# Attention for batches 1 to 3 by halves of 64 tokens, with head and token on the partitions

## The chip, the cores and the metric

The kernel runs on one core of a Trainium2 chip. The metric is device time in microseconds (us) of one execution, the median of several; the profile is of one execution taken by the hardware profiler. The engines are named PE (TensorE: matrix products, its weight loads shown apart as PEld), DVE (VectorE), ACT (ScalarE), POOL (GpSimd) and SP (SyncE, which here issues all DMAs). Each engine works through its own queue in order; they meet at semaphores.

## The reference

q, k and v have 4 batches, 8 heads, 768 tokens and 64 dimensions per head, in fp32. Per head h there is a decay gamma = 1 - 2^(-5-h) and a recurrent state of 64 x 64:

```
state = gamma * state + k[t]^T v[t]
y[t]  = (1/8) * q[t] state
```

The eight heads' y are laid side by side (512 columns, 3072 rows of all batches), and a feed-forward stage follows: h = relu(y @ w_in) with 2048 columns, out = (h * h) @ w_out, 512 columns, fp32.

## The kernel before

The recurrence is done in chunks of C = 128 tokens, 24 in all (`chunks`, six per batch). q is scaled by gamma^t/8 and k by gamma^(-t) (`scale_q` L241, `scale_kv` L252), so that inside a batch the state is a plain sum. Heads go in pairs (NPAIR = 4): two heads of 64 dimensions fill the 128 partitions. For one chunk:

- `load_q`, `load_kv` (L78 to L91): DMAs from SP bring q for two chunks, and k and v for one, with tokens on the partitions: one DMA for k and one for v, 256 KB each.
- k is scaled on DVE into `ks`, v is cast on POOL into `v_bd`.
- q and k are transposed so that the dimensions of a pair lie on the partitions: for chunks below DMA_FROM = 8 by PE (L272, L286), from 8 on by DMAs (`dma_transpose_q` L300, `dma_transpose_k` L308). k is then put into a block-diagonal tile `k_bd`, one head of a pair in each half of the partitions (for DMA transposes by DVE, `spread_k` L314).
- `scores` (L323): two halves of four products each, k tokens x q tokens of one head (128 x 128), into PSUM tile `st`; DVE multiplies by the causal mask into `pt`.
- `state` (L347): four products (one per pair) add this chunk's k^T v to `c_ps`, a PSUM tile that lives through a batch; ACT and DVE each copy one half of the diagonal blocks into `s_bd`. The last chunk of a batch has none.
- `outputs` (L374): per pair one product with the state before the chunk (not in a batch's first chunk) and one per head with `pt`, twelve products into PSUM tile `y`; one ACT copy brings it into `xt` (L399).

All of these products have 128 moving columns. The feed-forward stage takes blocks of chunks (BLOCKS, four chunks and then two at a time) in pieces. A block of two has eight pieces of the first product (`first_product` L416, relu by ACT L428, square by DVE L412) and eight of the second (L478; every fourth ends with ACT's copy L488 and a store by SP L490). The pieces are numbered through the program. `put` hangs a step of attention on a piece's number, its place, and `before` (L611) emits the steps of a place right after that piece, then the squares that are due. So the order in every queue is written out by hand. `attend` (L573) gives the places of one chunk; for chunks from 8 on they are d-13 (scaling, k's transpose, load of chunk m+3), d-7, d-5, d-3 and d (outputs), with d = 55, 62, 70, then every 8 pieces; q's scaling and transposition come at d-15 or d-16. Places 33 to 40, 49 to 56, 65 to 72 and so on follow pieces of the first product, those between follow pieces of the second. PSUM has eight banks: one each for `tp`, `st`, `y` and `c_ps`, four for the feed-forward stage. At the start, before the first feed-forward work can run, `keep_awake` (L221) fills PE with idle products of 512 or 64 columns, each with its own weight load.

Of the kernel before, what the change touches and what calls it, by code (L numbers as in the profile page):

```python
# [20 lines left out]

DMA_FROM = 8


@with_exitstack
def kernel(
# [9 lines left out]
    nc = tc.nc  # L36
# [23 lines left out]
    qkpool = ctx.enter_context(tc.tile_pool(name="qkpool", bufs=4))  # L60
    qTpool = ctx.enter_context(tc.tile_pool(name="qTpool", bufs=3))
    kTpool = ctx.enter_context(tc.tile_pool(name="kTpool", bufs=2))
    ptpool = ctx.enter_context(tc.tile_pool(name="ptpool", bufs=2))
    xtpool = ctx.enter_context(tc.tile_pool(name="xtpool", bufs=2))
    hpool = ctx.enter_context(tc.tile_pool(name="hpool", bufs=2))
    wstage = ctx.enter_context(tc.tile_pool(name="wstage", bufs=5))
# [19 lines left out]
    def load_kv(m):  # L86
        b, i = chunks[m]
        for name, src, to in (("kn", k, raw_k), ("vn", v, raw_v)):
            t = ldpool.tile([P, H, D], FP32, name=name)
            nc.sync.dma_start(t[:], src[b, :, i * C : (i + 1) * C, :].rearrange("h s d -> s h d"))  # L90
            to[m] = t  # L91
# [33 lines left out]
    for h in range(H):  # L125
        nc.gpsimd.memset(lng[:, h : h + 1], float(np.log(gammas[h])))

    def exponents(pattern, step, name):
        ex_i = const.tile([P, NCH, H], I32, name=f"{name}_i")
        nc.gpsimd.iota(ex_i[:], pattern=pattern, base=0, channel_multiplier=step)  # L130
        ex_f = const.tile([P, NCH, H], FP32, name=f"{name}_f")
        nc.vector.tensor_copy(ex_f[:], ex_i[:])
        nc.vector.tensor_tensor(
            out=ex_f[:],
            in0=ex_f[:],
            in1=lng[:, None, :].to_broadcast([P, NCH, H]),
            op=ALU.mult,
        )
        return ex_f


    ex_q = exponents([[2 * C, NCH // 2], [1, 2], [0, H]], 2, "ex_q")
    ex_k = exponents([[C, NCH], [0, H]], 1, "ex_k")
    qf = const.tile([P, NCH, H], FP32)
# [27 lines left out]
    )  # L172


    v_bds = [const.tile([P, NPAIR, 4, D], BF16, name=f"v_bd{j}") for j in range(4)]
    k_bds = [const.tile([P, NPAIR, 2, C], BF16, name=f"k_bd{j}") for j in range(2)]
    s_bds = [const.tile([P, NPAIR, 2, D], BF16, name=f"s_bd{j}") for j in range(2)]
    def zero_on_scalar(out, rows=slice(0, P)):
# [59 lines left out]
    at = {m: {} for m in range(NCHUNK)}  # L238
    xts = {}

    def scale_q(m):  # L241
# [65 lines left out]

    def dma_transpose_k(m):  # L308
        a = at[m]
        kT = kTpool.tile([P, NPAIR, C], BF16, name="kT")  # L310
        nc.sync.dma_start_transpose(kT[:], a["ks"].rearrange("s h d -> s (h d)"))
        a["kT"] = kT

    def spread_k(m):  # L314
        a = at[m]
        kT = a.pop("kT")
        k_bd = k_bds[m % 2]
        for hh in range(2):
            rows = slice(64 * hh, 64 * (hh + 1))
            nc.vector.tensor_copy(k_bd[rows, :, hh, :], kT[rows])  # L320
        a["k_bd"] = k_bd

    def scores(m, half, pool=ps_st, name="st"):  # L323
# [23 lines left out]
    def state(m, on_scalar=1):  # L347
# [18 lines left out]
        for hh in range(2):  # L366
# [3 lines left out]
            else:  # L370
                nc.vector.tensor_copy(s_bd[rows, :, hh, :], c[rows, :, hh, :])

    def outputs(m):
        b, i = chunks[m]  # L374
        a = at.pop(m)
        tb = block_of[m]
        if m == first[tb]:
            xts[tb] = xtpool.tile([P, NCB, BLOCKS[tb] * C], BF16, name="xt")
        off = (m - first[tb]) * C
        y = ps_y.tile([P, NPAIR, C], FP32, name="y")  # L380
# [23 lines left out]

    squares = []

    def take_squares():
        while squares:  # L410
            hv = squares.pop(0)
            nc.vector.tensor_mul(hv, hv, hv)  # L412

    h2s = {}

    def first_product(tb, hp, f, cols):  # L416
# [16 lines left out]
    def first_unit(tb, g, c, parts=(0, 1)):  # L433

        if tb not in h2s:
            h2s[tb] = hpool.tile([P, NFB, 4 * C], BF16, name="h2")
        if (tb, g, c) not in open_ps:
            open_ps[tb, g, c] = ps_f.tile([P, FPQ, C], FP32, name="psf")
        hp = open_ps[tb, g, c]
        cols = slice(c * C, (c + 1) * C)  # L440
        half = FPQ // 2
        for part in parts:
            for fq in range(part * half, (part + 1) * half):
                first_product(tb, hp[:, fq, :], g * FPQ + fq, cols)
        if 1 in parts:
            relu(h2s[tb][:, g * FPQ : (g + 1) * FPQ, cols], open_ps.pop((tb, g, c)))

    def ffn_pieces(tb):
        nch = BLOCKS[tb]
        TB = nch * C  # L450
        if tb == 0:
            for f in range(FPQ, NFB):
                hp = ps_f.tile([P, TB], FP32, name="psf")
                first_product(tb, hp[:], f, slice(0, TB))
                relu(h2s[tb][:, f, :], hp)
                yield
# [6 lines left out]
        else:  # L463
            h2s[tb] = hpool.tile([P, NFB, 4 * C], BF16, name="h2")
            per = 512 // TB
            for f0 in range(0, NFB, per):
                hp = ps_f.tile([P, per, TB], FP32, name="psf")
                for f in range(f0, f0 + per):
                    first_product(tb, hp[:, f - f0, :], f, slice(0, TB))
                relu(h2s[tb][:, f0 : f0 + per, :TB], hp)  # L470
                yield

        h2 = h2s.pop(tb)

        def second(op, j, g, cols=slice(0, DM)):
            for fq in range(FPQ):
                f = g * FPQ + fq
                nc.tensor.matmul(  # L478
                    op[:],
                    lhsT=h2[:, f, j * C : (j + 1) * C],  # L480
                    rhs=w_out_bf[g][:, fq, cols],
# [4 lines left out]
        def store(op, j, cols=slice(0, DM)):  # L486
            osb = opool.tile([P, cols.stop - cols.start], FP32, name=f"osb{cols.stop - cols.start}")
            nc.scalar.activation(osb[:], op[:], AF.Copy)  # L488
            r0 = (first[tb] + j) * C
            nc.sync.dma_start(out[r0 : r0 + C, cols], osb[:])  # L490

# [80 lines left out]

    def attend(m, scaled, places):  # L573
        by_dma = m >= DMA_FROM
        if m % 2 == 0:
            put(scaled, scale_q, m)
            put(scaled if by_dma else places[0], dma_transpose_q if by_dma else transpose_q, m)
        put(places[0], scale_kv, m)
        if by_dma:
            put(places[0], dma_transpose_k, m)  # L580
        put(places[1], spread_k if by_dma else transpose_k, m)
        put(places[2], scores, m, 0)
        put(places[3], scores, m, 1)
        put(places[3], state, m)
        put(places[4], outputs, m)

    put(6, load_w_out, 2)
# [10 lines left out]
    attend(5, None, (27, 29, 31, 33, 35))  # L598
    attend(6, 30, (33, 35, 37, 39, 42))
    attend(7, None, (40, 42, 44, 46, 49))  # L600

# [4 lines left out]
    for m, d in zip(range(8, NCHUNK), done):  # L606
        attend(m, d - 15 if d < 70 else d - 16, (d - 13, d - 7, d - 5, d - 3, d))
        if m + 3 < NCHUNK:
            put(d - 13, load, m + 3)
# [43 lines left out]
```

## Time and profile before

| | us |
|---|---|
| median of 3 runs (221.71 to 222.68) | 221.72 |
| the profiled execution | 221.87 |
| its span, first to last instruction | 220.1 |
| PE busy | 211.2 |
| DVE busy | 127.0 |
| ACT busy | 116.4 |
| POOL busy | 30.6 |

The profiled execution's own time is 1.8 us longer than its span. The granted TensorE clock was full in every stretch. In a row of the timeline the columns are start, length, engine, line, operation, what is written from what, how many neighbours are merged, and in brackets the idle time of the engine before it with what ended it. In a row of the table by stretches each engine's busy time is followed by its number of instructions; the last three columns are the granted clock, the DMA share and GB/s. DVE's scaling of k takes 716 ns, its mask 692 ns, its square 437 ns; ACT's relu takes 596 ns, the copy into `xt` 746 ns; ACT's state copy takes 373 ns and DVE's 427 ns; POOL's cast of v 662 ns. A k transposition by DMA lands 2.4 us after its issue, one of q 4.3 us.

### The profile page before, as it was taken

To read this page: it belongs to the slowest core of one execution; us is meant where nothing else is said; L and a number is where in the kernel's file an instruction comes from. 1 tells how busy PE (TensorE), PEld (TensorE's weight loads), DVE (VectorE), ACT (ScalarE), POOL (GpSimd) and SP (SyncE) were. 2 spreads that over 40 slices of the span, in tenths; PEclk is the share of its full clock that TensorE was granted. 3 is DMA by queue.
4 is the path that set the end of the run, shared out by engine and by line. 5 is a ranking of instruction groups with operands and counts; after the bars stand their busy time and mean duration, and the time that the engine had idled before them with its cause. 6 is when DMAs were issued, how large, how long until landed. Compare 5 with 4: busy or idle time off the path is not lost.

```text
span 220.1 us, 4737 instructions
## 1 busy us (share of the span) xinstructions
PE 211.2 (96%) x1920; PEld 148.9 (68%) x1943; DVE 127.0 (58%) x257; ACT 116.4 (53%) x206; POOL 30.6 (14%) x66
## 2 busy tenths in 40 slices
PE   6798999999999999999999999999999999999994
PEld 1466744556975975875975975975975975975853
DVE  4857789362495683682783783782783783751320
ACT  8564788338853653652653643652643643642631
POOL 3213435542111110101100101100101000000000
PEclk9999999999999999999999999999999999999999
DMA  6999999999998996397395398396398222201102
GB/s 152 238 231 369 388 374 232 362 246 216 288 236 132 259 157 132 115 231 155 99 228 136 114 209 182 87 236 155 93 209 191 71 51 71 74 0 48 51 0 95
DMA packets 87925, 38.05 MB, mean 173 GB/s; under 512 B 67808, under 2 KB 81376, under 8 KB 87904
## 3 DMA queue, kind: packets, MB, share of 16 engines
q1 hardware_dynamic: 87904, 37.76, 73.0%
q8 instruction: 15, 0.25, 0.5%
q14 instruction: 6, 0.05, 0.1%
HBM read 27.26 MB, written 6.29 MB: 152 GB/s over the span
## 4 chain that ended last, share of the span: by engine, by line
PE 92%; DMA 2%; ACT 1%; SPq 1%; DVE 1%; issue 1%; ACTq 0%
PE psf L419 38%; PE psf L478 37%; PE y L391 5%; PE st L331 4%; DMA kn<-in_k_dram 2%; PE y L383 2%; PE c_ps L357 2%; SPq L90 1%; PE psf L226 1%; PE tp L277 1%; PE tp L290 1%; DVE ks L255 1%; ACT xt L399 0%; PE psf L331 0%; PE y L226 0%
## 5 line engine op out<-in xcount | busy, mean ns | idle before, releaser
L419 PE MATMUL psf<-xt,w_in_bf 128*128 128x256 bf16 (+2 forms) x879 | 91.3, 259 | 0.6 <-ACT xt L399 0.4
L478 PE MATMUL psf<-w_out_bf,h 128*128 128x512 bf16 (+2 forms) x378 | 88.5, 370 | 1.0
L419 PEld LDWEIGHTS <-w_in_bf 128*128 128x128 bf16 x880 | 72.4, 98 | 13.6 <-issue 0.5
L428 ACT ACTIVATE h<-psf 128x512 bf16<-128x512 f32 x96 | 57.0, 596 | 26.1 <-PE psf L419 24.8
L478 PEld LDWEIGHTS <-h 128*128 128x128 bf16 x400 | 37.0, 98 | 34.5
L338 DVE TENSOR_TENSOR pt<-st,cmask 128x512 bf16<-128x512 f32 x44 | 30.4, 692 | 42.8 <-PE st L331 42.2
L412 DVE TENSOR_TENSOR h<-h 128x512 bf16<-128x512 bf16 x96 | 40.9, 437 | 23.9 <-ACT h L428 22.4
L263 POOL CAST v_bd<-vn 128x512 bf16<-128x512 f32 x24 | 15.9, 662 | 127.2 <-DMA vn<-in_v_dram 123.4
L488 ACT ACTIVATE osb<-psf 128x512 f32<-128x512 f32 (+2 forms) x25 | 14.4, 580 | 27.4 <-PE psf L478 24.3
L399 ACT ACTIVATE xt<-y 128x512 bf16<-128x512 f32 x24 | 17.9, 746 | 19.0 <-PE y L391 18.3
L331 PEld LDWEIGHTS <-k_bd 128*128 128x128 bf16 x192 | 14.1, 98 | 7.3 <-ACT k_bd L297 1.2
L391 PE MATMUL y<-pt,v_bd 128*128 128x128 bf16 x192 | 18.2, 219 | 0.0
L369 ACT ACTIVATE s_bd<-c_ps 64x256 bf16<-64x256 f32 x24 | 9.0, 373 | 17.2 <-PE c_ps L357 16.9
L331 PE MATMUL st<-qT,k_bd 128*128 128x128 bf16 x176 | 17.5, 220 | 0.5 <-DVE k_bd L295 0.5
L255 DVE TENSOR_TENSOR ks<-kn,kf 128x512 bf16<-128x512 f32 x24 | 17.2, 716 | 0.2
L391 PEld LDWEIGHTS <-v_bd 128*128 128x128 bf16 x192 | 14.5, 98 | 2.4 <-issue 0.7
L244 DVE TENSOR_TENSOR qs<-qn,qf 128x1024 bf16<-128x1024 f32 x12 | 15.0, 1253 | 1.4 <-DMA qn<-in_q_dram 1.4
L320 DVE COPY k_bd<-kT 64x512 bf16<-64x512 bf16 x32 | 9.1, 286 | 10.4 <-DMA kT<-ks 9.9
L383 PE MATMUL y<-qT,s_bd 128*128 128x128 bf16 x80 | 14.5, 219 | 0.1
L226 PE MATMUL psf<-ident 128*128 128x512 bf16 (+1 forms) x48 | 8.8, 326 | 2.1 <-POOL ident L152 2.1
L297 ACT ACTIVATE k_bd<-tp 64x512 bf16<-64x512 bf16 x12 | 7.0, 587 | 4.7 <-PE tp L290 4.5
L383 PEld LDWEIGHTS <-s_bd 128*128 128x128 bf16 x80 | 7.8, 98 | 1.2
(45 smaller groups left out, 78.9 us busy)
## 6 DMA issues: line engine op xcount, KB each, us to landing
qn<-in_q_dram SPq DMA_DIRECT2D x12, 512.0 KB, 4.7
kn<-in_k_dram SPq DMA_DIRECT2D x24, 256.0 KB, 5.1
vn<-in_v_dram SPq DMA_DIRECT2D x24, 256.0 KB, 5.5
out_dram<-osb SPq DMA_DIRECT2D x23, 256.0 KB, 3.3
w_stage<-in_moe_w_out_dram SPq DMA_DIRECT2D x4, 1024.0 KB, 10.2
w_stage<-in_moe_w_in_dram SPq DMA_DIRECT2D x3, 1024.0 KB, 10.9
w_stage<-in_moe_w_in_dram SPq DMA_DIRECT2D x2, 512.0 KB, 6.5
kT<-ks SPq DMA_TRANSPOSE x16, 2.4
```

Of the source, the lines that this page charges most:

```text
L244: nc.vector.tensor_tensor(out=qs[:], in0=raw_q.pop(m).rearrange("s h r d -> s r h d"), in1=qf[:, i : i + 2, :, None].to_broadcast([P, 2, H ...
L255: nc.vector.tensor_tensor(out=ks[:], in0=raw_k.pop(m)[:], in1=kf[:, i, :, None].to_broadcast([P, H, D]), op=ALU.mult,)
L263: nc.gpsimd.tensor_copy(v_bd[:, :, ::3, :], vn.rearrange("s (p hh) d -> s p hh d", hh=2))
L331: nc.tensor.matmul(st[:, pp, hh, :], lhsT=a["k_bd"][:, p, hh, :], rhs=a["qT"][:, :, p, :], start=True, stop=True,)
L338: nc.vector.tensor_tensor(out=a["pt"][:, 2 * half : 2 * half + 2], in0=st[:], in1=cmask.rearrange("s r t -> s (r t)")[:, None, None, :].to ...
L383: nc.tensor.matmul(y[:, p, :], lhsT=s_bds[(m - 1) % 2][:, p], rhs=a["qT"][:, :, p, :], start=True, stop=False,)
L391: nc.tensor.matmul(y[:, p, :], lhsT=a["v_bd"][:, p, 2 * hh : 2 * hh + 2, :], rhs=a["pt"][:, p, hh, :], start=(i == 0 and hh == 0), stop=(h ...
L399: nc.scalar.activation(xts[tb][:, :, off : off + C].rearrange("e p (s r) -> e p r s", r=2), y.rearrange("e p (r s) -> e p r s", r=2), AF.Copy,
L412: nc.vector.tensor_mul(hv, hv, hv)
L419: nc.tensor.matmul(hp, lhsT=w_in_bf[g][:, cb, fq * 128 : (fq + 1) * 128], rhs=xts[tb][:, cb, cols], start=(cb == 0), stop=(cb == NCB - 1),)
L428: nc.scalar.activation(hv, hp[:], AF.Relu)
L478: nc.tensor.matmul(op[:], lhsT=h2[:, f, j * C : (j + 1) * C], rhs=w_out_bf[g][:, fq, cols], start=(f == 0), stop=(f == NFB - 1),)
```

## The change

It concerns chunks 6 to 23, which are batches 1 to 3. The loads of k and v put token and head of a pair together on the partitions: partition 64 * hh + s holds token s of a half chunk for head hh of each pair, and the free dimension counts half u and pair p (eight groups of 64). That takes four DMAs of 64 KB for k and four for v. A chunk is then worked in two halves u of 64 tokens:

- `scale_k2`: two DVE instructions, one for each half of the partitions, write the scaled k into a block-diagonal tile `ks_bd2s`; its other blocks were zeroed once.
- `cast_v2`: three POOL casts, one into `v2` and one for each half of the partitions into the block-diagonal `v_bd2s`.
- `transpose_k2`: the block-diagonal k is transposed whole, eight blocks of 128 x 128: by one DMA from chunk 8 on, by PE for chunks 6 and 7, with one copy by ACT and one by DVE. `spread_k` is gone.
- `scores2`: eight products of 64 columns into one `st`, one mask on DVE.
- `state2`, once for each half: four products of 64 columns, then the two copies into `s_bd`, of which there are now three.
- `outputs2`, once for each half: eight products of 64 columns (four in a batch's first half) and one ACT copy of that half. Both halves stand at one place and write one PSUM tile `y`.

Constants for it are made at place 8 (`pack_constants`), and ten zeroings on DVE stand at places 10 to 19. The tile of h is cut into tiles of 4096 columns, three buffers for the former two of twice the size.

```diff
-    hpool = ctx.enter_context(tc.tile_pool(name="hpool", bufs=2))
+    hpool = ctx.enter_context(tc.tile_pool(name="hpool", bufs=3))
...
+                pairs = rows.rearrange("(p hh) (u s) d -> hh s u p d", hh=2, u=2)
+                for hh in range(2):
+                    for u in range(2):
+                        nc.sync.dma_start(
+                            t[64 * hh : 64 * (hh + 1), u * NPAIR : (u + 1) * NPAIR, :],
+                            pairs[hh, :, u],
+                        )
...
+    def zero_off_diagonal(t, hh):
+        nc.vector.memset(t[halves[hh], :, 1 - hh, :], 0.0)
...
+    def scale_k2(m):
+        b, i = chunks[m]
+        ks = ks_bd2s[m % 2]
+        kn = raw_k.pop(m)
+        for hh, rows in enumerate(halves):
+            nc.vector.tensor_tensor(
+                out=ks[rows, :, hh, :],
+                in0=kn[rows],
+                in1=kf2[rows, i].rearrange("s u p -> s (u p)")[:, :, None].to_broadcast(
+                    [64, 2 * NPAIR, D]
+                ),
+                op=ALU.mult,
+            )
+        at[m]["ks"] = ks
+
+    def cast_v2(m):
+        vn = raw_v.pop(m)
+        v2 = v2pool.tile([P, 2 * NPAIR, D], BF16, name="v2")
+        nc.gpsimd.tensor_copy(v2[:], vn[:])
+        v_bd = v_bd2s[m % 2]
+        for hh, rows in enumerate(halves):
+            nc.gpsimd.tensor_copy(v_bd[rows, :, hh, :], vn[rows])
+        at[m].update(v2=v2, v_bd=v_bd)
+
+    def transpose_k2(m):
+        a = at[m]
+        kT = kTpool.tile([P, 2 * NPAIR, C], BF16, name="kT")
+        if m >= DMA_FROM:
+            nc.sync.dma_start_transpose(kT[:], a["ks"].rearrange("s c hh d -> s (c hh d)"))
+        else:
+            tp = ps_tp.tile([P, 2 * NPAIR, C], BF16, name="tp")
+            for c in range(2 * NPAIR):
+                nc.tensor.transpose(tp[:, c, :], a["ks"][:, c], ident[:])
+            nc.scalar.activation(kT[:, 0:NPAIR], tp[:, 0:NPAIR], AF.Copy)
+            nc.vector.tensor_copy(kT[:, NPAIR:], tp[:, NPAIR:])
+        a["kT"] = kT
+
+    def half_of(qT, p, u):
+        return qT[:, :, p, u * (C // 4) : (u + 1) * (C // 4)]
+
+    def scores2(m):
...
+        for u in range(2):
+            for p in range(NPAIR):
+                c = u * NPAIR + p
+                nc.tensor.matmul(
+                    st[:, c, :], lhsT=kT[:, c, :], rhs=half_of(a["qT"], p, u),
...
+        nc.vector.tensor_tensor(out=pt[:], in0=st[:], in1=cmask2..., op=ALU.mult)
+
+    def state2(m, u):
...
+        for p in range(NPAIR):
+            nc.tensor.matmul(
+                c[:, p, :],
+                lhsT=a["ks"][:, u * NPAIR + p],
+                rhs=a["v2"][:, u * NPAIR + p, :],
...
+        s_bd = s_bds[(2 * m + u) % 3]
+        nc.scalar.activation(s_bd[halves[0], :, 0, :], c[halves[0]], AF.Copy)
+        nc.vector.tensor_copy(s_bd[halves[1], :, 1, :], c[halves[1]])
+
+    def outputs2(m, u):
...
+        if u == 0:
+            xt_of(m)
+            a["y"] = ps_y.tile([P, NPAIR, 2, C // 2], FP32, name="y")
+        y = a["y"]
...
+        for p in range(NPAIR):
+            inter = i > 0 or u > 0
+            if inter:
+                nc.tensor.matmul(
+                    y[:, p, u, :],
+                    lhsT=s_bds[(2 * m + u - 1) % 3][:, p],
+                    rhs=half_of(a["qT"], p, u),
...
+            nc.tensor.matmul(
+                y[:, p, u, :],
+                lhsT=a["v_bd"][:, u * NPAIR + p],
+                rhs=a["pt"][:, u * NPAIR + p, :],
...
+        nc.scalar.activation(
+            xts[tb][:, :, off : off + C // 2].rearrange("e p (s r) -> e p r s", r=2),
+            y[:, :, u, :].rearrange("e p (r s) -> e p r s", r=2),
+            AF.Copy,
+        )
...
+    def attend2(m, q_at, places):
+        attend_q(m, *q_at)
+        put(places[0], scale_k2, m)
+        put(places[0], cast_v2, m)
+        put(places[1], transpose_k2, m)
+        put(places[2], scores2, m)
+        put(places[3], state2, m, 0)
+        put(places[4], state2, m, 1)
+        for u in range(2):
+            put(places[5], outputs2, m, u)
...
-    attend(6, 30, (33, 35, 37, 39, 42))
-    attend(7, None, (40, 42, 44, 46, 49))
+    put(8, pack_constants)
+    for j, t in enumerate(ks_bd2s + v_bd2s):
+        for hh in range(2):
+            put(10 + 2 * j + hh, zero_off_diagonal, t, hh)
+    for hh in range(2):
+        put(18 + hh, zero_off_diagonal, s_bds[2], hh)
+    attend2(6, (30, 32), (32, 35, 38, 39, 40, 42))
+    attend2(7, (None, None), (39, 42, 45, 46, 47, 49))
...
-        attend(m, d - 15 if d < 70 else d - 16, (d - 13, d - 7, d - 5, d - 3, d))
+        q_at = (d - 15 if d < 70 else d - 16,) * 2
+        attend2(m, q_at, (d - 13, d - 13, d - 5, d - 4, d - 2, d))
```

## The prediction

> **What bounds the kernel now.** I read the page's engine totals and its chain of waits first: is one engine the limit, and where? PE (matrix products) is busy 96% and makes up 92% of the chain. So a change counts by what it takes from PE's queue and by any moment for which PE stops.
>
> ```profile
> span 220.1 us, 4737 instructions
> PE 211.2 (96%) x1920; PEld 148.9 (68%) x1943; DVE 127.0 (58%) x257; ACT 116.4 (53%) x206; POOL 30.6 (14%) x66
> PE 92%; DMA 2%; ACT 1%; SPq 1%; DVE 1%; issue 1%; ACTq 0%
> ```
>
> Next the table by stretches of 10 us, for the stage that the change rewrites. PE has no idle time there (its 78 to 96 records are long products); DVE is at half to two thirds.
>
> ```profile
> 120.00:130.00 10.00, 9.90 (x96) 8.38 (x96) 6.96 (x15) 6.47 (x12) 0.61 (x1) 1.00 0.70 178
> 130.00:140.00 10.00, 9.95 (x78) 6.35 (x77) 4.62 (x10) 3.29 (x7) 1.23 (x2) 1.00 0.87 160
> ```
>
> Then the timeline, for the pace of PE. A row merges neighbours and holds the drain of the last one (0.22 us for 128 columns, 0.19 for 64; the shortest rows). Four products of 128 columns: (0.39 - 0.22)/3 = 56 ns each. The warm-up products of 64 columns, each with its own weight load: (0.86 - 0.19)/23 = 29 ns. So 64 columns cost half of 128, loads included.
>
> ```profile
> 13.64 0.86 PE L226 MATMUL psf<-ident 128*128 128x64 bf16 x24
> 132.06 0.39 PE L331 MATMUL st<-qT,k_bd 128*128 128x128 bf16 x4
> ```
>
> Last, two places where two engines read different parts of one PSUM tile. The transposes end at 15.11; ACT copies one half of `tp` at 15.15; DVE, idle for 1.34 us, starts on the other half at 15.78, after ACT's end, and ACT is named as releaser. The second pair does the same on disjoint partitions. No data passes between them: in this program accesses of different engines to one PSUM bank go one after the other, whatever columns they touch.
>
> ```profile
> 14.49 0.62 PE L277 MATMUL tp<-ident,qs 128*128 128x128 bf16 x8
> 15.15 0.60 ACT L280 ACTIVATE qT<-tp 128x512 bf16<-128x512 bf16 x1 [0.56 <-PE tp L277]
> 15.78 0.42 DVE L281 COPY qT<-tp 128x512 bf16<-128x512 bf16 x1 [1.34 <-ACT qT L280]
> ...
> 17.36 0.59 ACT L297 ACTIVATE k_bd<-psf 64x512 bf16<-64x512 bf16 x1 [1.61 <-PE psf L290]
> 17.98 0.43 DVE L295 COPY k_bd<-psf 64x512 bf16<-64x512 bf16 x1 [1.18 <-ACT k_bd L297]
> ```
>
> **The change, part by part.** It concerns chunks 6 to 23, three batches of six.
>
> *PE's own work.* Before: scores 8 x 18, state 4 x 15, outputs 12 x 18 - 4 x 3 = 408 products of 128 columns, at 56 ns 22.8 us. After: scores2 8 x 18, state2 8 x 18 - 4 x 3, outputs2 16 x 18 - 4 x 3 = 552 of 64 columns, at 29 ns 16.0 us. Chunks 6 and 7 have four more transposes each, 8 x 56 ns = 0.4 us. All of it is on the path: -6.4 us. Bounds: 27 ns a product (half of 56 less a little) gives -7.5; 56 ns gives +8.5.
>
> The Trainium skill speaks against this in "TensorE: Matmul & The Clock Gate", section Back-to-back issue gap: in streams of weight load and product the load shares in the pace, and 128 columns sustain about 81 ns. The trace disagrees (56 ns with loads, 29 ns for 64 columns). By an estimate from that page's figure, 552 products at 81 ns would take 44.7 us, and the sum below would be 266.
>
> *outputs2: two halves in one bank, at one place.* `y` is one tile of 512 fp32, a bank. Half 0's eight products write it, ACT copies half 0, then half 1's eight products write other columns of the same bank. By the rows above PE must wait for ACT's copy, and nothing else in PE's in-order queue can go ahead. The copy of half the columns: 128x512 takes 0.746 us, ACT's 64x256 from PSUM 0.373; half of the former plus its share of fixed cost is 0.45 (from 596 and 373 ns for 512 and 256 elements the fixed part is 0.15; the strided rest 0.6 halves to 0.3). Bounds 0.37 and 0.75.
>
> ```profile
> 85.82 0.22 PE L383 MATMUL y<-qT,s_bd 128*128 128x128 bf16 x1
> 86.69 0.74 ACT L399 ACTIVATE xt<-y 128x512 bf16<-128x512 f32 x1 [1.80 <-PE y L391]
> ...
> 94.13 0.22 PE L383 MATMUL y<-qT,s_bd 128*128 128x128 bf16 x1
> 94.33 0.60 ACT L428 ACTIVATE h<-psf 128x512 bf16<-128x512 f32 x1 [0.28 <-PE psf L419]
> 95.00 0.75 ACT L399 ACTIVATE xt<-y 128x512 bf16<-128x512 f32 x1
> ```
>
> At 85.82 (a place in the second products) ACT is free: eight products 0.20, drain 0.19, ACT's start 0.04, copy 0.45, PE's start 0.05, against 0.23 without the wait: 0.70 us. At 94.13 (first products) the relu of the piece just done is ahead on ACT until 94.93: copy 95.00 to 95.45, PE at 95.50 instead of 94.36: 1.14 us, say 1.1. Places 49, 55, 70, 86 ... (nine) lie in first products, 42, 62, 78, 94 ... (nine) in second: 9 x 1.1 + 9 x 0.7 = +16.2 us. Bounds 14.8 and 21.6 by the copy's; 0 if PE doesn't wait.
>
> *state2: two passes over one accumulator.* Pass 1 adds to the PSUM columns that pass 0's copies are reading, so PE must wait for both copies, ACT's 0.373 then DVE's 0.427; before, a whole chunk (8 us) lay between. Passes stand two pieces apart (1.75 us), one in chunks 6 and 7. DVE's queue decides. In an even chunk, from PE's arrival at scores2: mask 0.44 to 1.13, both scale_k2 of the next chunk to 2.56, a square to 3.00, DVE's state copy to 3.43. PE reaches pass 1 at 0.23 + 0.87 + 0.12 + 1.75 = 2.97 and goes on at 3.48: 0.5 us. In an odd chunk there is no square and PE arrives at 2.93; DVE's copy ends at 2.99: 0.1. Sum 8 x 0.5 + 5 x 0.1 (the last chunk of a batch has no pass 1) + 2 x 0.3 (chunks 6 and 7: drain 0.19, copies 0.37 + 0.11 + 0.43, less a piece of 0.86) = +5.1 us. Bounds 0 (copies always in time) and +16 (rival below).
>
> *DVE and ACT otherwise.* DVE a chunk: one mask instead of two (-0.69), no spreading of k (-0.57), scale_k2 two instructions of 64 partitions and the same length (+0.72), one state copy more (+0.43): even. ACT: 0.45 x 2 instead of 0.75, one state copy more: +0.5 of 8 us. Both stay under 70%: nothing beyond the waits above.
>
> *POOL:* three casts of 0.61 instead of one, 1.8 of 8 us; they wait for loads and freed buffers, not for PE. Nothing, unless beside DVE (rival).
>
> *SP and DMA.* SP issues per block of two chunks 16 loads instead of 4, and k transposes of q's size. Before a block takes 16.6 us, after about 18. Issues: k 2 x 1.5 (like q's 1.5), q's own 1.5 + 0.57, two stores 0.36 each, loads 16 x 0.33 (the shortest store) to 0.57 (the median k load): 11.1 to 14.9 us. It fits. A kT lands like qT, 4.3 us (3.1 to 5.5) after issue instead of 2.4; it is issued some 2.6 us after its place, scores2 needs it eight pieces later (8 us): covered by about 1 us. Nothing; if the cover goes, the wait is one for one.
>
> *Setting up, places 8 to 19.* pack_constants is small operations on idle POOL (1.78 us idle at 27.07) and 0.5 us of DVE. The ten memsets, 8 x 0.27 + 2 x 0.14 = 2.4 us, go into DVE just where it runs without a break (31.99 to 37.39), ahead of the scaling of q for chunk 4.
>
> ```profile
> 38.04 1.22 DVE L244 TENSOR_TENSOR qs<-qn,qf 128x1024 bf16<-128x1024 f32 x1
> 40.32 0.61 PE L277 MATMUL tp<-ident,qs 128*128 128x128 bf16 x8
> ```
>
> That ends at 39.26 and PE takes it at 40.32; 2.2 us later less 0.3 of idle time, PE waits about +0.9 us. Bounds 0 and 1.5.
>
> The tiles of h are cut in halves and use three buffers: no wait on them before, none after, 0.
>
> Sum: -6.4 + 16.2 + 5.1 + 0.9 = +15.8. The profiled execution took 221.87 (span 220.1 and 1.8 around it): 237.7. The median of the runs is 0.15 lower: 237.5.
>
> **The rivals.**
>
> *PE doesn't wait in outputs2* (accesses of PE and ACT to different columns of a bank are let run together). The rows show ACT against DVE, none shows a PE write against a reader of other columns. Then 237.5 - 16.2 = 221.3, no change; if the state copies are in time too, 216. It is the other side, and decides where each of the 18 waits is under 0.02 us (0.3 us with the state waits gone). Chance 0.10. The Trainium skill, "PSUM — Partial Sum Buffer", section PSUM bank collisions raise a hardware error, wants PSUM guarded by bank and 32-partition group, not by address; by that rule the wait stays, as both halves use all partitions.
>
> *DVE is late because POOL casts beside it.* At 39.17 a k scaling took 1.10 us instead of 0.68 beside a POOL cast. Twice 0.42 for the 13 chunks with a scaling ahead of the state copy: +10.9, 248. Against: POOL's buffers come free six pieces earlier, so the casts should be over. Chance 0.06.
>
> *SP becomes the bound.* At 133.09 a k load took 0.84 us to issue; 16 x 0.84 + 5.8 = 19.2 a block against 18.1: 8 x 1.1, 246. It decides from 0.77 us an issue. Against: 0.57 and 0.53 where nothing is queued. Chance 0.05.
>
> *Products of 64 columns take as long as 128* (the weights then set the pace): 8.5 instead of -6.4, 252. Against: the 24 warm-up products; for: these all loaded one matrix. Chance 0.05.
>
> **How the numbers follow.** The forecast has 0.74, and 237.5 is its time. Its range by the bounds is 229 to 244 (state waits gone and copies of 0.37 us: 231, memsets hidden and 27 ns a product as well: 229; copies of 0.75 us and 1.5 us at the memsets: 243.5). I give 228 to 245; left out are the first rival and those above 245, under 2 in 10 with what the forecast has in its own tails. What tells from no change is about 0.5%, 1.1 us. The first rival, spread over 216 to 224, gives faster 0.05 and same 0.04; the forecast's tail 0.01 of each. Slower 0.89.
>
> **What would show it.** Right: PE idle 0.7 or 1.1 us between the two halves of each chunk's outputs, released by ACT's xt copy; smaller idle time before state2's second pass, released by DVE's s_bd copy; 64-column products 29 ns apart; loads of k and v issued in 0.35 to 0.6 us. Wrong: ACT's copy of half 0 overlapping half 1's products, PE waiting for kT, or a wait before the transposes at 40 us that isn't there.

## The result and the profile after

The changed kernel takes 241.82 us (median of four runs, 241.61 to 243.74) where the kernel before, measured beside it, takes 221.74: a ratio of 1.0914 (95% interval 1.0852 to 1.0976). It is slower, as forecast, and 4.3 us above the forecast of 237.5, inside the range of 228 to 245.

The profiled execution took 241.61 us, with a span of 239.5 and 2.1 us around it. So the span grew by 19.4 us, and what lies around it by 0.3. The page's totals and its chain of waits, the first views that were read of the kernel before:

```profile
span 239.5 us, 5316 instructions
...
PE 212.8 (89%) x2095; PEld 145.4 (61%) x2095; DVE 130.4 (54%) x257; ACT 123.1 (51%) x241; POOL 57.9 (24%) x115
...
PEclk9999999999999799999999999999999999999999
...
PE 74%; ACT 10%; DVE 9%; DMA 4%; issue 2%; ACTq 0%; DVEq 0%
```

PE fell from 96% to 89% busy and from 92% to 74% of the chain. No other engine of this line filled up, but the issuing of DMAs, which is SP's work, isn't counted in it; the rest of the chain is now handed from engine to engine. Two of the 10 us stretches in the rewritten stage say the same (columns: the stretch and its length; then busy us with the number of records of PE, PEld, DVE, ACT, POOL; granted clock; DMA share; GB/s). PE, which had no idle time in such stretches, now stands still for about 1 us in 10:

```profile
140.00:150.00 10.00, 9.15 (x85) 5.56 (x85) 4.64 (x9) 4.04 (x9) 2.49 (x4) 1.00 0.84 193
150.00:160.00 10.00, 8.93 (x100) 7.49 (x99) 6.33 (x12) 6.10 (x12) 2.70 (x4) 1.00 0.59 147
```

The list of waits names what for (total us, times, the longest). Those for `y`, the state copies and q had been forecast, that for kT had not:

```profile
PE y L539 <- ACT xt L553: 12.3, 18, 0.9
PE st L488 <- DMA kT<-ks_bdp: 3.6, 2, 3.4
PE c_ps L515 <- DVE s_bd L525: 2.3, 8, 0.4
...
PE tp L323 <- DVE qs L290: 1.6, 3, 0.8
```

These figures leave out the time in which a product's drain overlaps its successor. Taken instead from the start of each product to the start of the next, less the product's usual pace, the span's growth comes apart like this:

| part | forecast us | measured us | from |
|---|---|---|---|
| PE's own products | -6.4 | -6.4 | counts times pace; 29 ns for 64 columns |
| `y`: PE waits for the copy of half 0 | +16.2 | +15.2 | 18 waits: 0.96 to 1.08 in first products, 0.70 in second |
| state2: second pass | +5.1 | +3.8 | 7 x 0.43, 0.56 at 64 us, 0.23 at 72 us; nothing in odd chunks |
| q of chunk 4 and the zeroing | +0.9 | +0.95 | one wait at 41.34 us |
| kT late | 0 | +3.9 | 3.5 at 79.95 us, 0.4 at 169.85 |
| clock behind the late kT | - | +1.6 | 4.0 us at a granted 0.60 |
| w_in at 33.7 us | - | +0.1 | one wait |
| sum | +15.8 | +19.2 | span: +19.4 |

The timeline shows the first of these waits in a place in first products and then one in second products (start, length, engine, line, operation, tiles; in brackets the idle time before it and what ended it). At 139.31 the eighth product of half 0 is issued, but ACT has a relu ahead of the copy of `y`; PE goes on at 140.31. At 148.14 ACT is free and PE goes on at 148.87:

```profile
139.31 0.60 ACT L597 ACTIVATE h<-psf 128x512 bf16<-128x512 f32 x1 [0.28 <-PE psf L588]
139.31 0.19 PE L546 MATMUL y<-pt,v_bdp 128*128 128x64 bf16 x1
...
139.80 0.45 ACT L553 ACTIVATE xt<-y 128x256 bf16<-128x256 f32 x1
140.31 0.19 PE L539 MATMUL y<-qT,s_bd 128*128 128x64 bf16 x1 [0.80 <-ACT xt L553]
```

```profile
148.14 0.19 PE L546 MATMUL y<-pt,v_bdp 128*128 128x64 bf16 x1
148.87 0.19 PE L539 MATMUL y<-qT,s_bd 128*128 128x64 bf16 x1 [0.54 <-ACT xt L553]
```

What had not been forecast lies at 80 us. The first of the following fences holds PE's rows in the timeline, the second the stretches around them:

```profile
75.54 1.06 PE L588 MATMUL psf<-xt,w_in_bf 128*128 128x128 bf16 x16
79.95 0.41 PE L488 MATMUL st<-qT,kT 128*128 128x64 bf16 x8 [3.35 <-DMA kT<-ks_bdp]
80.19 1.36 PE L588 MATMUL psf<-xt,w_in_bf 128*128 128x128 bf16 x16
```

```profile
76.60:80.00 3.40, 0.05 (x2) 0.06 (x3) 0.00 (x0) 0.60 (x1) 0.45 (x1) 1.00 0.82 170
80.00:84.00 4.00, 4.00 (x51) 4.00 (x52) 1.87 (x4) 1.35 (x3) 0.00 (x0) 0.60 0.41 90
```

PE stands still for 3.4 us until the transposed k of chunk 8 lands. Then its clock is granted at a mean of 0.60 over 4 us: the same sixteen products take 1.36 us instead of 1.06, and 4.0 x 0.40 = 1.6 us are lost after the wait is over. In the Trainium skill, "TensorE: Matmul & The Clock Gate", Part 1 on the HAM clock gate, PE goes to half its clock after an idle window of about 3.4 us and comes back after about as long a time of sustained work; the trace agrees with it, with an idle time of 3.4 us and half the clock from 80.75 to 84.2 us, 3.5 us in all. The 3.4 us aren't a sharp bound in these runs, though: in the run with half 1 a place later the clock also fell to half at a wait of 2.6 us, and it stayed there for 6.9 us.

Why kT is late is seen in SP's queue. Its rows in one block of two chunks:

```profile
139.08 1.31 SPq L468 DMA_TRANSPOSE kT<-ks_bdp  x1
140.44 0.60 SPq L87 DMA_DIRECT2D qn<-in_q_dram  x1
141.10 2.62 SPq L102 DMA_DIRECT2D kn<-in_k_dram  x4
143.82 2.59 SPq L102 DMA_DIRECT2D vn<-in_v_dram  x4
146.52 1.26 SPq L349 DMA_TRANSPOSE qT<-qs  x1
147.89 1.24 SPq L468 DMA_TRANSPOSE kT<-ks_bdp  x1
149.17 2.92 SPq L102 DMA_DIRECT2D kn<-in_k_dram  x4
152.19 3.09 SPq L102 DMA_DIRECT2D vn<-in_v_dram  x4
155.38 1.02 SPq L658 DMA_DIRECT2D out_dram<-osb  x2
156.50 1.33 SPq L468 DMA_TRANSPOSE kT<-ks_bdp  x1
```

Each row begins within about 0.1 us of the end of the one before it. From one kT at 139.08 to the one two chunks later at 156.50 SP needs 17.4 us, and the sixteen loads of 64 KB take 11.2 of them, 0.70 each. Over five blocks, from kT of chunk 9 at 85.46 to that of chunk 19 at 174.51, it needs 17.8 us a block; a block of PE's takes 17.9, and from 21 to 193 us SP never pauses for more than 0.44 us. Its queue is full. In the kernel before it wasn't: here SP pauses for 1.0 us ahead of qT and 1.8 us ahead of kT, which leaves at once when its k is scaled (148.40):

```profile
141.98 0.57 SPq L90 DMA_DIRECT2D kn<-in_k_dram  x1
142.65 1.36 SPq L90 DMA_DIRECT2D vn<-in_v_dram  x1
144.98 1.69 SPq L303 DMA_TRANSPOSE qT<-qs  x1
148.42 1.39 SPq L311 DMA_TRANSPOSE kT<-ks  x1
```

In the changed kernel the scaling of the k that the transpose at 147.89 moves had ended at 145.58. In 14 of the 16 chunks from chunk 8 on, kT leaves 0.1 to 0.2 us after SP's last instruction. In twelve of them that is 2 to 3 us after its data was ready, in chunk 8, the first whose k is transposed by DMA, 6.5 us, and in chunk 9 10.6 us. So SP, not the scaling, sets when k is transposed.

### The profile page after: what moved, and what is told of

It reads as the page before. It is cut to its first block, busy times and chain, and to the rows that moved or that the text cites. A ratio compares the mean times of both kernels' runs of the same rounds, so it can differ in the third digit from the quotient of the medians.

```text
span 239.5 us, 5316 instructions
## 1 busy us (share of the span) xinstructions
PE 212.8 (89%) x2095; PEld 145.4 (61%) x2095; DVE 130.4 (54%) x257; ACT 123.1 (51%) x241; POOL 57.9 (24%) x115
## 4 chain that ended last, share of the span: by engine, by line
PE 74%; ACT 10%; DVE 9%; DMA 4%; issue 2%; ACTq 0%; DVEq 0%
PE psf L646 32%; PE psf L588 29%; ACT h L597 5%; ACT xt L553 3%; DMA kT<-ks_bdp 3%; PE y L539 2%; PE c_ps L515 2%; PE st L488 2%; DVE h L568 2%; DVE qs L290 2%; DVE s_bd L525 2%; DMA qn<-in_q_dram 2%; PE y L546 1%; PE y L425 1%; PE tp L323 1%
## 5 line engine op out<-in xcount | busy, mean ns | idle before, releaser
L495 DVE TENSOR_TENSOR pt<-st,cmask 128x512 bf16<-128x512 f32 x18 | 12.4, 691 | 40.0 <-PE st L488 39.5
L461 POOL CAST v_bdp<-vn 64x512 bf16<-64x512 f32 x36 | 23.5, 653 | 40.8 <-PE y L546 39.7
L458 POOL CAST v<-vn 128x512 bf16<-128x512 f32 x18 | 13.3, 739 | 81.9 <-issue 56.0
L553 ACT ACTIVATE xt<-y 128x256 bf16<-128x256 f32 x36 | 16.3, 454 | 20.3 <-PE y L546 20.3
L445 DVE TENSOR_TENSOR ks_bdp<-kn,kf 64x512 bf16<-64x512 f32 x36 | 25.9, 719 | 0.6
L539 PE MATMUL y<-qT,s_bd 128*128 128x64 bf16 x132 | 12.1, 192 | 12.3 <-ACT xt L553 12.3
L525 DVE CAST s_bd<-c_ps 64x256 bf16<-64x256 f32 x33 | 14.1, 428 | 11.4 <-ACT s_bd L524 10.7
L524 ACT ACTIVATE s_bd<-c_ps 64x256 bf16<-64x256 f32 x33 | 12.3, 372 | 14.2 <-PE c_ps L515 14.1
L546 PEld LDWEIGHTS <-v_bdp 128*128 128x128 bf16 x144 | 9.7, 97 | 15.3 <-issue 14.0
L546 PE MATMUL y<-pt,v_bdp 128*128 128x64 bf16 x144 | 12.9, 193 | 0.0
L515 PE MATMUL c_ps<-v,ks_bdp 128*128 128x64 bf16 x132 | 9.3, 194 | 2.4 <-DVE s_bd L525 2.3
```

The source lines that it names most:

```text
L445: nc.vector.tensor_tensor(out=ks[rows, :, hh, :], in0=kn[rows], in1=kf2[rows, i].rearrange("s u p -> s (u p)")[:, :, None].to_broadcast([6 ...
L461: nc.gpsimd.tensor_copy(v_bd[rows, :, hh, :], vn[rows])
L515: nc.tensor.matmul(c[:, p, :], lhsT=a["ks"][:, u * NPAIR + p], rhs=a["v2"][:, u * NPAIR + p, :], start=(i == 0 and u == 0 and p == 0), sto ...
L525: nc.vector.tensor_copy(s_bd[halves[1], :, 1, :], c[halves[1]])
L539: nc.tensor.matmul(y[:, p, u, :], lhsT=s_bds[(2 * m + u - 1) % 3][:, p], rhs=half_of(a["qT"], p, u), start=True, stop=False,)
L546: nc.tensor.matmul(y[:, p, u, :], lhsT=a["v_bd"][:, u * NPAIR + p], rhs=a["pt"][:, u * NPAIR + p, :], start=not inter, stop=True,)
```

## The experiments

All edits are to the changed kernel, except where the kernel before is named. Ratios are to the kernel before, measured beside each, with 95% intervals.

**Half 1 of the outputs in a bank of its own.** The second half of `y` takes a buffer from the pool of `tp`, so that no product writes to a bank that ACT is reading.

```diff
-            a["y"] = ps_y.tile([P, NPAIR, 2, C // 2], FP32, name="y")
-        y = a["y"]
+            y = ps_y.tile([P, NPAIR, 2, C // 2], FP32, name="y")
+        else:
+            y = ps_tp.tile([P, NPAIR, 2, C // 2], FP32, name="tp")
```

> Half 1 of each chunk's outputs is written into the bank of tp, half 0 stays in y; nothing else differs from the changed kernel. Theory (PE waits because both halves lie in one PSUM bank): the 18 waits for ACT's xt copy, 15.3 us in the changed kernel's trace, go, and the time falls to 241.8 - 15.3 = 226.5 us (225 to 228). Rival (ACT is simply late there, and PE would wait for it at the next step that needs it): the idle time moves to another line and the time stays within 5 us of 241.8.

Measured: 238.23 us, ratio 1.0728 (1.0672 to 1.0785). The 18 waits for ACT's copy are gone, but only 3.6 of their 15.2 us came off the time. The line of the waits, and one chunk in the timeline, SP's row and PE's:

```profile
PE st L488 <- DMA kT<-ks_bdp: 12.5, 11, 3.8
```

```profile
154.41 1.02 SPq L659 DMA_DIRECT2D out_dram<-osb  x2
155.54 1.32 SPq L468 DMA_TRANSPOSE kT<-ks_bdp  x1
159.90 0.41 PE L488 MATMUL st<-qT,kT 128*128 128x64 bf16 x8 [1.27 <-DMA kT<-ks_bdp]
```

PE now waits for kT in 11 chunks, 14.3 us from start to start. The chunk shown had its k scaled by 152.57; the transpose left at 155.54, when SP had issued the loads and stores ahead, and PE had its scores at 159.90. The mechanism of the wait is as forecast; its price in this kernel isn't, because SP's queue takes as long as before: from kT of chunk 9 to that of chunk 19 it is 89.1 us, with the `y` waits and without them. A wait of 0.8 us is new: chunk 7's transposes, which use the bank of `tp`, wait for ACT's copy out of it.

**Half 1 a place later.** The same wait is removed in another way: a piece of the feed-forward stage's products, some 0.9 us, is put between the two halves. In chunks 6 and 7, half 1 then reads the v of chunks 8 and 9, which is cast into the same tile by then, so those parts of the output are others.

```diff
-            put(places[5], outputs2, m, u)
+            put(places[5] + u, outputs2, m, u)
```

> Both halves in one bank as in the changed kernel, but half 1 one piece of feed-forward work (0.87 us) after half 0. Theory: the wait is as long as ACT's copy and the relu ahead of it, 0.7 to 1.1 us, so a piece in between hides nearly all of it: 15.3 us shrink to 0 to 2, 227 us (226 to 229). Rival (two separate groups of eight small products cost PE something of their own, whatever lies between): 235 us or more.

Measured: 237.95 us, ratio 1.069 (1.0641 to 1.0738). Of the `y` waits two of 0.2 us are left; PE waits for kT in nine chunks, 11.4 us, and 1.9 us for POOL's casts of the v of chunks 8 and 9. Two edits that have only the removed wait in common end within 0.3 us of each other, with waits for kT in its place.

**One load later.** If the loads ahead of it in the queue make kT of chunk 8 late, moving one set of them back should bring it in time.

```diff
-    for m, place in ((8, 26), (9, 31), (10, 36)):
+    for m, place in ((8, 26), (9, 31), (10, 43)):
```

> The loads for chunk 10 are issued at place 43 instead of 36, behind chunk 8's k transpose. Theory (at 80 us PE waits 3.5 us for kT because SP issues nine loads ahead of the two transposes of chunk 8): the wait goes, and with it the stretch at reduced clock behind it (about 1.7 us): 241.8 - 5 = 236.8 us (235.5 to 238.5). Rival (the transpose itself is slow, 1024 packets among other transfers): the wait stays over 2 us, 241 us.

Measured: 243.48 us, ratio 1.0934 (1.0877 to 1.0991), no gain but 1.7 us more. The wait at 80 us is gone, and kT of chunk 9 is late by as much: one wait of 4.7 us at 90.3 us, behind the loads of chunks 11 and 10. The queue holds more in this stretch than it can issue; another order moves the wait to another chunk. That the late kT is behind the loads is borne out; that there was room for them seven places on is not.

**The second state pass a place later.**

```diff
-    attend2(6, (30, 32), (32, 35, 38, 39, 40, 42))
-    attend2(7, (None, None), (39, 42, 45, 46, 47, 49))
+    attend2(6, (30, 32), (32, 35, 38, 39, 41, 42))
+    attend2(7, (None, None), (39, 42, 45, 46, 48, 49))
...
-        attend2(m, q_at, (d - 13, d - 13, d - 5, d - 4, d - 2, d))
+        attend2(m, q_at, (d - 13, d - 13, d - 5, d - 4, d - 1, d))
```

> The second pass of state2 stands one place later (d-1 instead of d-2). Theory (PE waits for the copies of pass 0, 0.43 us in even chunks, 3.8 us in all): the wait goes, 241.8 - 3.8 = 238 us (237 to 239.5). Rival (the copies then delay ACT's xt copy, which stands one piece behind, and the wait in outputs grows by as much): 241 us or more.

Measured: 239.62 us, ratio 1.0777 (1.0723 to 1.0831). All waits for the state copies are gone (3.8 us); the `y` waits (15.3) and that for kT stay. 2.2 us came off the median, not 3.8; in the profiled execution 1.05 us of waiting for the cast of w_in at 34 us had appeared, ahead of all that was edited. That wait adds up to between 0 and 1.6 us in these kernels, and what sets it is not shown.

**Two banks, and the v loads on ACT.** If it is the issuing on SP that makes kT late, another queue must cure it; if it is the transfers themselves, it must not.

```diff
-                        nc.sync.dma_start(
+                        (nc.sync if name == "kn" else nc.scalar).dma_start(
```

(and the two banks as above)

> Two banks for the halves of y as in e2, and the four loads of v of chunks 6 to 23 are issued by ACT's queue instead of SP's. Theory (with the outputs' wait gone, SP's 18 us of issuing per block of two chunks set the pace, and kT is late for that reason alone): SP falls to about 13 us a block, the waits for kT (14.3 us in e2) go, and the time falls from 238.2 to 223 to 226 us; ACT pays 2.6 us a chunk for the issues, and some relus come late. Rival (the k transpose lands late because of its 1024 packets and the transfers around it): the waits for kT stay over 8 us, 234 us or more.

Measured: 244.28 us, ratio 1.0945 (1.0861 to 1.1029). No wait for kT is left, the transposes leave 0.1 us after their data is ready: the transfers are not the cause. But the median is the longest of all. ACT's rows, and then the product that waits for it, show the main reason:

```profile
139.39 4.21 ACTq L102 DMA_DIRECT2D vn<-in_v_dram  x4
143.65 0.60 ACT L598 ACTIVATE h<-psf 128x512 bf16<-128x512 f32 x1 [3.72 <-DMA vn<-in_v_dram]
```

```profile
145.03 0.37 PE L515 MATMUL c_ps<-v,ks_bdp 128*128 128x64 bf16 x4 [2.76 <-DVE s_bd L525]
```

ACT issues the four loads of a chunk in 2.6 us at the median, 4.2 us in the longest case, which is shown, and begins no other work meanwhile; the relu and the state copies queue up behind, and PE waits 14.1 us for those copies. It also waits 4.4 us for ACT's casts of w_out at 40 and 48 us, and loses another 5.5 us at half its clock behind the three longest waits. Whether the 4.2 us are the issuing itself or a wait inside it, the trace doesn't say.

**Two banks, and the v loads on POOL.** The same with `nc.gpsimd`, an engine whose own work is 24% of the span.

```diff
-                        nc.sync.dma_start(
+                        (nc.sync if name == "kn" else nc.gpsimd).dma_start(
```

> As e6, but the loads of v are issued by POOL. Theory (SP's issuing is the bound): the same as e6, 222 to 226 us, without ACT's part. Rival (the transposes' own transfer is the bound): 234 us or more.

Measured: 223.26 us over ten runs, ratio 1.0041 (1.0014 to 1.0067), as SP's queue as the cause has it. From chunk 10 on kT leaves 0.1 us after its k is scaled, and PE has no wait for it.

**One bank, and the v loads on POOL.** It is the fourth corner of a square.

> The changed kernel with one edit: POOL issues the loads of v of chunks 6 to 23; both halves of y stay in one bank. Theory (SP's queue makes kT late at 80 us, and the outputs' wait hides SP's lateness elsewhere): the wait for kT and the stretch at reduced clock go (3.9 + 1.7 us), the 18 waits of the outputs stay at 15.3 us: 241.8 - 5.6 = 236.2 us (235 to 238). Rival (the loads by POOL are what made e7 fast, the outputs' wait matters little): near e7, below 229 us.

Measured: 237.48 us, ratio 1.0677 (1.0641 to 1.0712). No kT waits, clock 1.000, the `y` waits 15.2 us from start to start as before. Medians in us:

| | v loads on SP | v loads on POOL |
|---|---|---|
| halves of `y` in one bank | 241.8 | 237.5 |
| halves of `y` in two banks | 238.2 | 223.3 |

The bank wait is worth 3.6 us in the left column and 14.2 in the right one; relieving SP is worth 4.3 us in the upper row and 15.0 in the lower. The kernel before, measured beside each, had medians of 221.7 to 222.7, so each of these differences is uncertain by about 1 us. Each wait covers the other. Taken by itself, either would look small.

**The kernel before, with its loads split.** The 256 KB loads of k and v for chunks 6 to 23 are issued as four of 64 KB, by quarters of the tokens, and nothing else is changed. So it is the number of issues alone.

```diff
+                for j in range(4):
+                    nc.sync.dma_start(t[32 * j : 32 * (j + 1)], rows[32 * j : 32 * (j + 1)])
```

> The kernel before with one part of the change alone: k and v of chunks 6 to 23 come in four DMAs of 64 KB each (by quarters of the tokens, layout as before). Theory (each issue costs SP 0.65 us whatever its size): SP goes from about 8.5 to 16.3 us of 16.6 a block, kT is issued up to 3 us later, and as it is wanted six pieces after its place the time rises by 0 to 4 us, 222 to 226. Rival (it is only k's larger transposes that fill SP and DMA): SP stays under 12 us a block and the time at 221.9 within 0.5 us.

Measured: 228.93 us, ratio 1.0283 (1.0222 to 1.0343), more than either theory had. In the later stage SP keeps up (0.51 us a load) and PE waits for nothing. All of the loss comes from one place, at which the changed kernel loses too, in the timeline and as a stretch:

```profile
75.01 1.23 SPq L316 DMA_TRANSPOSE kT<-ks  x1
...
77.84 0.82 PE L336 MATMUL st<-qT,k_bd 128*128 128x128 bf16 x4 [4.74 <-DVE k_bd L325]
```

```profile
77.84:84.10 6.26, 6.22 (x58) 6.04 (x59) 4.13 (x9) 1.57 (x3) 0.62 (x1) 0.50 0.73 189
```

One wait of 4.7 us for the k of chunk 8, the first that is transposed by DMA, then 6.26 us at a granted clock of 0.50, 3.1 us more. Together 7.8 us; the profiled execution is 7.7 us longer than that of the kernel before, the median 6.2. The block-diagonal layout is not needed for this loss, four issues for one suffice.

**The zeroings later.** They are put at places 29 to 44, where DVE has idle time.

```diff
-    for j, t in enumerate(ks_bd2s + v_bd2s):
+    for t, place in zip((ks_bd2s[0], v_bd2s[0], ks_bd2s[1], v_bd2s[1], s_bds[2]), (29, 32, 36, 40, 43)):
...
+            put(place + hh, zero_off_diagonal, t, hh)
```

> The changed kernel with the ten zeroings of the block-diagonal tiles at places 29 to 44 instead of 10 to 19. Theory (they delay DVE's scaling of q for chunk 4, for which PE waits 0.95 us at 41 us): that wait goes and the time falls by 0.9 us to 240.9; if DVE's later steps are delayed instead, it stays at 241.8.

Measured: 241.72 us, ratio 1.0888 (1.0852 to 1.0925), no gain. The wait at 41 us, 0.95 us, is gone, so its cause was the zeroing as forecast. The wait for kT at 80 us grew from 3.5 to 4.6 us, and a state copy is 0.5 us late at 71 us. PE came earlier to a point that SP's queue sets: the scores behind that wait start at 79.88 us, in the changed kernel at 79.95.

**All cures in one.** `y` is laid out by pair, parity and then token, so that both halves fill one tile and one ACT instruction copies it after half 1; the second state pass and the zeroings are moved as above; POOL issues the v loads.

```diff
-                    y[:, p, u, :],
+                    y[:, p, :, u * (C // 4) : (u + 1) * (C // 4)],
...
-        nc.scalar.activation(
-            xts[tb][:, :, off : off + C // 2].rearrange("e p (s r) -> e p r s", r=2),
-            y[:, :, u, :].rearrange("e p (r s) -> e p r s", r=2),
-            AF.Copy,
-        )
...
+            nc.scalar.activation(
+                xts[tb][:, :, off : off + C].rearrange("e p (s r) -> e p r s", r=2),
+                y[:],
+                AF.Copy,
+            )
```

> The changed kernel with four edits: both halves of y are copied by one ACT instruction after half 1, the second pass of state2 stands at d-1, the loads of v are issued by POOL, the zeroings stand at places 29 to 44. Theory (the change's products save 6.4 us, and all the rest is waits that these edits take away): 222 - 6.4 + 1, 216 to 218.5 us, faster than the kernel before. Rival (a further bound shows up when these waits go, as SP's did in e2): 221 us or more.

Measured: 219.31 us, ratio 0.9856 (0.9819 to 0.9893). That is 1.4% faster than the kernel before, and 0.8 us above the upper end of what was expected. What is left is 1.2 and 0.4 us at w_in at 34 us and 1.1 and 0.8 us at kT. Ahead of the first, POOL issues loads and then casts w_out while DVE is in the exponents of the decay:

```profile
28.56 2.61 POOL L102 DMA_DIRECT2D vn<-in_v_dram  x4
30.86 1.54 DVE L150 TENSOR_TENSOR ex_k_f<-ex_k_f,lng 128x48 f32<-128x48 f32 x1
31.14 1.75 POOL L257 CAST w_out_bf<-w_stage 128x512 bf16<-128x512 f32 x3
...
34.30 0.39 PE L589 MATMUL psf<-xt,w_in_bf 128*128 128x512 bf16 x1 [1.00 <-ACT w_in_bf L251]
```

**The same, with POOL issuing v from chunk 8 on only.**

```diff
-                        (nc.sync if name == "kn" else nc.gpsimd).dma_start(
+                        (nc.gpsimd if name == "vn" and m >= 8 else nc.sync).dma_start(
```

> As e14, but POOL issues the loads of v from chunk 8 on only; those of chunks 6 and 7 stay with SP. Theory (in e14 PE waits 1.6 us at 34 us for w_in, because two small DVE operations of the constants, 0.2 to 0.3 us in the kernel before, take 0.60 and 1.54 us while POOL issues those loads): that wait goes and the time falls from 219.3 to 217.5 to 218.5 us. Rival (the wait comes from w_in's late landing): 219.3 within 0.5.

Measured: 217.94 us, ratio 0.982 (0.9791 to 0.9849). This version is 1.8% faster than the kernel before. The wait at 34 us is gone; since that wait comes and goes between kernels, one trace doesn't prove that POOL's early issuing had made it. The totals and a stretch of the later stage:

```profile
span 216.2 us, 5265 instructions
...
PE 206.7 (96%) x2095; PEld 142.8 (66%) x2095; DVE 134.3 (62%) x257; ACT 120.0 (56%) x223; POOL 102.7 (48%) x179
```

```profile
130.00:140.00 10.00, 10.00 (x96) 6.62 (x94) 5.32 (x11) 4.74 (x9) 5.70 (x10) 1.00 0.91 188
```

PE is without idle time again, and it has less to do: a block takes 15.5 to 15.8 us in this stage, 16.1 to 16.6 in the kernel before. The shorter products are worth 6.4 us; 1.6 and 0.8 us are left at kT (82 and 68 us). -6.4 + 2.4 = -4.0, against -3.8 in the medians.

**The kernel before, with the v loads on POOL from chunk 8.** Was relief of SP alone what the last version gained by?

```diff
+            (nc.gpsimd if name == "vn" and m >= 8 else nc.sync).dma_start(
```

> The kernel before with one edit: POOL issues the loads of v from chunk 8 on. Theory (the gain of e14 over the kernel before is the 6.4 us of shorter products, and SP was no bound before): no change, 222 within 0.7 us. Rival (it is the relief of SP that makes e14 fast): 220 us or less.

Measured: 224.1 us, ratio 1.0082 (1.0056 to 1.0108): 0.8% slower, by more than the theory that holds had allowed. Relief of SP by itself gains nothing here. The profiled execution is 1.5 us longer than that of the kernel before: PE waits 1.0 us for `k_bd` at 73.8 us and 0.2 at 114.8, the start-up takes 0.1 longer, and 0.2 us more lies outside the span. These are read from one trace and were not tested singly, so that POOL's issuing is what costs them is not shown.

## Why the prediction was right, and where it was off

- *PE's own work, -6.4:* right in size. The 64-column products come 29 ns apart with a different matrix each time too, so the rival of weight loads setting the pace falls. So does the Trainium skill's figure in "TensorE: Matmul & The Clock Gate", section Back-to-back issue gap: no run here shows 81 ns, 128 columns come 56 ns apart, loads included.
- *outputs2, +16.2:* right in mechanism, and 1.0 us too much. All 18 waits are there, and the copy took 0.45 us as estimated. The places in first products took 0.96 to 1.08 us instead of 1.1. The rival in which PE doesn't wait falls. Whether the order holds because of the bank or because of the tile was not tried.
- *state2, +5.1:* right in mechanism, 1.3 us too much: 0.43 instead of 0.5 in the even chunks, nothing instead of 0.1 in the odd ones. The rival with POOL's casts beside DVE falls; the two k scalings took 1.39 us together (0.72 each, and 0.72 is in the forecast), not 0.42 more each.
- *Setting up, +0.9:* 0.95, and the run without the early zeroings has no wait there.
- *SP and DMA, 0:* this is the step that failed. It took 0.33 to 0.57 us for an issue, from a store and a whole 256 KB load; a load of 64 KB took 0.61 at the median and 0.70 on the mean of the block shown. The sum of 11.1 to 14.9 us a block should have been 17.4 there: 11.2 for loads, 5.4 for the rest, 0.8 between them, for which it had no term. So it doesn't fit: at 17.8 us a block on the mean SP's queue is full, though the issues stay under the 0.77 us at which the rival was to decide. What stands last in a full queue leaves 2 to 3 us late. In most chunks the cover of kT just held, as it landed 3.5 us after its issue instead of 4.3. At chunk 8, whose transposes stand behind the loads that were placed ahead, kT left 6.5 us late: there the cover is gone, and at chunk 18 it was short by 0.4, 3.9 us in all. The 1.6 us of reduced clock behind it had no term at all.
- *What the sum could not see:* its terms add up in this kernel, within 0.2 us of the span, once kT is in. As prices of a repair they don't: without the `y` waits SP's queue sets the block at nearly the same time, so 15.2 us of waits were worth 3.6. The rival "SP becomes the bound", which had 0.05, holds beside the forecast: SP's queue alone keeps the kernel at 238.2 us, the `y` waits alone at 237.5.
- *The chances:* what the range leaves out was said to have under 2 in 10; the first rival and the three above 245 add up to 0.26.

So the time came out near the forecast by the forecast's main mechanism, with two terms 1.0 to 1.3 us too high, and one of 5.5 us left out. That the queue, which the forecast had at nothing, would by itself have led to nearly the same time is luck: the time alone doesn't confirm the mechanism, the 18 waits in the trace do.

## What to carry to other kernels

When a tile is cut into halves, give each half a PSUM buffer of its own or copy the whole once: a product that waits for a read of its own tile's other half costs PE 0.7 to 1.1 us here, more than the shorter products saved. Count DMA issues by queue and by period, with a row of the same size, and look at what stands last in a queue that is nearly full; bytes say little. Where two waits lie in the same period, undo them together before judging either: here they were worth 3.6 and 4.3 us singly and 18.6 together.

## What the runs showed of the hardware that was not expected

- A load of 64 KB costs its queue about as much as one of 256 KB: at the median 0.45 us (kernel before, split by tokens) and 0.61 (changed kernel), against 0.57 for a k load of 256 KB before.
- A single wait of 3.4 us costs PE another 1.6 to 1.7 us by the reduced clock behind it, one of 4.7 us (kernel before, split) another 3.1.
- It matters whose queue a load stands in: four v loads take 2.6 us of issuing on SP and on ACT and 2.4 on POOL at the median, but on ACT they stand in the way of the relus and copies (244.3 us), on POOL of little (223.3).
- A DVE instruction on 128x48 took 1.54 us beside POOL's cast of w_out (all cures in one), 0.54 and 0.65 beside such a cast in two other kernels (the changed one, and the one with POOL issuing v from chunk 8 on), and 0.21 where no cast ran (the zeroings later). POOL's issuing isn't enough for it: with two banks and the v loads on POOL it took 0.21 while POOL issued. What stretches it is only read from these traces, and 0.58 us in the kernel with one bank and the v loads on POOL, where a cast begins just as it ends, doesn't fit the casts alone.
